# An attention and gated long-convolution kernel: the order of its first loads, tile-wise loads of later batches, and a new written-out order

## The chip, the cores and the metric

The kernel runs on one core of one Trainium2 chip, as one program. The metric is the device time of one execution in microseconds. The core has five engines that run side by side, each through its own list of instructions in order: TensorE (PE in the profile, its weight loads PEld), VectorE (DVE), ScalarE (ACT), GpSimd (POOL) and SyncE (SP). GpSimd and SyncE issue most of the transfers here; a transfer that changes the type from fp32 to fp16 on its way is issued by GpSimd, one that copies as it is by SyncE.

## The reference, cut to what matters

Four batches of 768 rows go through attention of 8 heads with 64 columns each, and then through a gated long convolution over the rows:

```python
scores = scale * q @ k^T + bias          # bias = -slope[head] * distance
keep   = (column < 8) | (0 <= row - column < 96)
a      = softmax(where(keep, scores, -1e9))
x      = a @ v                           # [4, 768, 8*64]
proj   = x @ w_proj                      # [4, 768, 3*512] -> x1, x2, x3
conv   = irfft(rfft(x2) * rfft(filter))  # along the 768 rows
out    = (x1 * conv * x3) @ w_out        # fp32
```

The inputs are fp32; the kernel computes in fp16 with fp32 sums.

## The kernel before

**Tiling.** A batch's attention works on four head pairs (0 to 3) and three column groups. `turned` (L623) transposes the q and the k of a head pair on TensorE, six 128-row tiles each, and copies them to QT and KT. `scores` (L651) makes a pair's scores of one group; in batch 0 the distances (the array `dg`) are multiplied in on TensorE ahead of them ("near"), in later batches the exponentials are multiplied with a mask on VectorE. ScalarE takes the exponential to E. `values` (L695) multiplies with v and normalizes into xn, `transpose_x` (L744) turns the result to xT, and `butterfly` (L764) makes the sums and differences that the transform needs. `gate` and `gates` make x1 and x3 and their product; `conv` (L867) does the projection of x2, the transforms as matmuls with sine tables, the product with the filter's spectrum, the way back, the product with the gates and the output projection, whose results go out by SyncE.

**The order.** Every operation is recorded in a graph with its predecessors (`Plan.op`). A text, `ORDER` (L41), then lists all of them by number and engine: `50V` is operation 50 on VectorE. The four digits behind a P are PSUM banks, and `i3b6` means three dummy matmuls into bank 6 that only keep TensorE busy. Each engine runs its own operations in the text's order, and nothing is moved at run time. Copies that can run on VectorE or ScalarE get their engine from the text too. So an operation that waits holds up all that stand behind it on its engine.

**The first loads.** `load_pair` (L336) loads q and k of a head pair. For batch 0 and pairs 0 and 1 SyncE loads them as fp32 into staging places of their own (parts of h1, h2 and pp) and a "cast" on VectorE copies them to qn and kn (L307). All other q and k loads are issued by GpSimd, one head at a time, 768 rows of 64 columns (96 KB as fp16). The layout of qn and kn is [128 rows, 4 pairs, 6 tiles, 2 heads, 64]. `load_run` and `load_rows` load v by tiles of 120 rows, `load_w` the projection's weights, and the filter is one load of 768 KB into g. GpSimd also makes row numbers (L382), the identity (L199 of a library) and the first step of the distances (`distances`, L514 to L523), whose place in GpSimd's list is behind its first five loads: k, k, q, q of heads and the filter. SyncE's list begins with q and k of pair 0 or 1 into pp, q into h1, the first v rows of batch 0 into X, and k into h2.

**Later batches.** `load_batch` (L1079) calls `load_pair` for the four pairs of the next batch, and `load_v`. A transpose of one pair can start when the two heads of that pair have landed.

Of the kernel before, what the change touches and what calls it, by code (L numbers as in the profile page):

```python
# [17 lines left out]
P = 128  # L18
NG = 8
KL = P - NG  # L20
# [24 lines left out]
106P01 29V 105A 68G 6V 35V 107A 156P67 88P4 8V 157A 31V 69G 89V 123A 124P01 120P45 70G 214V 215V 71G 102P67  # L45
100P2 121A 74G 158P45 216V 103A 125A 249G 98P3 101V 154P67 159A 99V 64S 235G 155A 108P23 126P45 110P67 217V
250G 160P01 218V 109A 127A 219V 111V 220V 112V 238G 161A 247G 75G 248G 115P23 128P45 133P67 227P0 113P1 116V
72G 83A 117V 134V 85A 129V 241G 225P2 237G 135V 118P3 162P67 130V 167P45 73G 114V 131P1 27A 228A 226A 81A 28V
80A 206P2 163V 223P0 164V 132A 168V 136P1 236G 165P6 240G 169V 221P7 119V 166V 84A 170P3 189V 245G 246G 137A
209V 82A 242G 224A 79A 146P6 150P1 152A 171V 229P45 239G 352P3 151P1 222A 188V 244G 243G 197V 213A 211A 76G  # L50
191V 353A 350P7 147P0 251G 231V 180P5 148V 184P3 198V 351A 153V 230A 149V 385P01 199V 190V 182A 363P67 200V
207V 476G 201V 386A 475G 364A 142P4 138P5 186A 340P0 259G 254G 338P1 232P67 212A 341A 192V 144V 193V 202V 233A
194V 387V 339V 143P3 210A 203V 185P4 140A 176P6 256G 252S 354P01 208A 145V 423P23 234A 187V 178V 196V 414P45
355A 415A 255G 344P7 342P6 195V 139P0 348P1 345V 257G 343V 424A 356V 365V 204V 141V 181P7 474G 349A 379P23
473G 357P45 346P6 347V 461G 462G 258G 472G 172P1 183V 177P0 358A 484G 376P45 417P67 380A 359V 174A 360P23 205V
179V 377A 274P1 425V 261P0 253S 418A 361A 381V 420P67 382P45 416V 362V 265P2 421A 383A 469G 275A 263P3 471G
264A 371P45 378V 419V 422V 366P67 384V 289P1 372V 367V 262A 173P3 373V 466G 287P0 266A 388P45 368V 175V 290A
389V 288A 291V 374P2 269P6 267P7 369P3 375A 270A 268A 278P0 276P2 370A 463G 279A 577P3 393P01 390V 277A 280P2
292V 578A 271V 575P7 272V 470G 394V 576A 426P45 273V 465G 281A 282P3 477G 283A 391P6 395V 431P01 396P7 392A
397A 701G 427V 588P23 480G 428V 301P4 432V 285V 433V 589A 429P5 468G 464G 284V 410P7 430A 467G 573P6 434P0  # L60
482G 610P23 406P5 302A 571P4 706G 590V 574A 611A 305P6 699G 435V 306A 286V 695G 297P0 298A 303P1 412A 572V
295P2 453V 293P4 299P3 452V 296A 307P6 481G 308A 694G 294A 304A 300V 485G 563P0 398P7 698G 402P6 585P23 408A
400A 455V 567P1 404A 310V 309V 607P45 407P7 586A 691G 454V 686G 311V 564A 568A 608A 403P6 569P2 411P3 405V
570A 440P6 399P1 456V 565P0 442A 312V 457V 582P45 409V 696G 478S 609V 458V 401V 566A 645P67 646A 693G 583A
436P2 459V 413V 499P0 639P67 640A 486P1 313V 692G 500A 479S 437P3 697G 460V 314V 438A 487A 587V 601P67 604P45
501P2 690G 483G 439V 444P3 315V 612V 602A 687G 605A 579P67 647V 648P01 709G 446A 502A 603V 448P4 642P23 580A
643A 584V 606V 688G 445P5 794P6 618P23 649A 641V 792P7 795A 447V 596P01 793A 644V 581V 597V 700G 450A 619V
503P5 504A 796P6 788P7 598V 613P01 620V 316V 591P23 800P5 614V 260G 689G 514P4 789A 449P7 797A 507P6 592V 615V
651P01 515A 801A 508A 593V 505P2 650V 317V 867P45 318V 506A 594P3 798P6 451V 868A 490P2 799A 595A 656P45 319V
657V 652V 802P7 488P6 491A 658V 803A 616P2 441P3 599P7 659P4 489A 617A 621P6 510V 492P5 653V 509V 600A 512P2  # L70
622A 443V 493A 511V 654P7 494P0 513A 320P6 495A 635P5 707G 321A 813P01 329P2 516V 496V 655A 660A 702G 870P67
869V 814A 637A 330A 636P4 517V 335P0 807P23 677V 638V 678V 871A 497V 808A 832P45 673P1 679V 790P6 520P7 680V
703S 627P2 833A 681V 532P3 704S 521A 632P7 815V 675A 873P45 631P1 533A 682V 791A 332P6 498V 874A 526P3 524P4
708G 629A 705G 633A 522P2 527A 525A 333A 518P1 674P5 834V 683V 875V 685V 336A 322S 523A 628P4 710G 530P6 531A
528P0 676V 684V 634V 519A 630V 323P5 835P23 809V 810P67 529A 804P01 726P4 324A 811A 836A 864P67 711P5 623P2
805A 535V 334S 331S 865A 534V 812V 715P3 536V 826P67 829P01 625A 712A 806V 537V 716A 713P5 830A 821P23 827A
837V 538V 872V 326P0 816P67 727A 737P4 539V 714A 822V 540V 823V 724P1 817V 327A 543V 818A 669P0 866V 541V
843P23 844V 738A 671A 828V 725A 728P5 717P4 729A 730P6 845V 665P7 718A 731A 831V 542V 719P1 739P0 624P5 720A
838P23 626V 740A 667A 670P6 325S 839V 840A 732P0 881P45 722V 672V 544V 876P67 733A 741V 819P1 661P2 662P0 877V
882V 878V 820A 721V 337S 560P1 883A 879P3 824P6 663A 735V 666P7 723V 884P4 548P2 825A 841P6 846P5 885A 742V  # L80
668V 734V 880A 664V 755P4 842A 736V 847A 747P3 557P7 756A 753P6 757P0 902V 751P4 328S 748A 903V 743P3 754A
749P5 758A 752A 905V 750A 745P6 746A 848P0 904V 744A 759V 545P4 852P3 554P6 906V 854A 911P3 546A 924P4 912A
760V 907V 551P3 549A 937P2 925A 850A 761V 908V 762V 849P4 939P0 909V 938A 910V 763V 561A 913P2 547S 851V 555A
764V 562S 940A 558A 914A 857P1 928P0 929A 917P2 915P7 918A 926P0 916A 919P2 927A 941V 920A 853P7 552A 765V
942V 930P0 932P6 766V 860P2 931A 768V 767V 550S 933A 922V 856P3 770P0 921V 858A 935V 553S 556S 923V 934V 773P3
771A 943P0 962P6 862A 774A 947P2 944A 948A 855V 936V 861P4 769V 963A 958P0 945P5 949P2 959A 964P3 863V 946A
950A 960P6 772S 776P0 779P2 965A 961A 859V 775S 777A 951V 952V 780A 967V 966V 953V 968V 785P6 954V 782P7 969V
559S 955V 890P2 898P3 970V 956V 778S 900A 971V 781S 887P0 957V 972V 894P1 886P3 973V 783A 892A 975V 974V 786A
976V 988V 896V 899P2 986V 977P6 978A 895P7 888A 983P1 897V 984A 784S 901V 787S 891P7 889V 980P6 981A 893V 979S
989V 985S 987V 999P6 993P7 1000A 982S 994A 1001S 995S 996P6 997V 990P0 998S 991A 992S  # L90
# [108 lines left out]
class Fused:  # L199
# [7 lines left out]
    LATE = frozenset(())  # L207
# [27 lines left out]
    def buffers(self):  # L235
# [5 lines left out]
        self.qn = t("qn", [P, 4, 6, 2, D])  # L241
        self.kn = t("kn", [P, 4, 6, 2, D])
# [32 lines left out]
        self.under = [[("h", 0), ("h", 2)], [("h", 1), ("h", 3)]] + [[(x, i) for x in ("p1", "p2") for i in range(2)]] * 2  # L275
        self.y = t("y", [P, 4, S])
# [43 lines left out]
    def load(self, eng, dst, src, w, nbytes, name, r=()):  # L320
        self.loads += 1
        e = {"G": self.nc.gpsimd, "S": self.nc.sync}[eng]
        return self.g.op(eng, 0.57 + 0.00035 * nbytes[0] if eng == "G" else 0.5, lambda _: e.dma_start(dst, src),  # L323
                         w=w, r=r, nbytes=nbytes, name=name, bias=-2000.0 + self.loads)
# [14 lines left out]
    def load_pair(self, b, hp):  # L339
        for i, (what, x, dst) in enumerate((("q", self.q, self.qn), ("k", self.k, self.kn))):  # L340
            to = dst[:, hp]
            if b or hp not in self.PLAIN:
                for hh in range(2):
                    self.load("G", to[:, :, hh], x[b, 2 * hp + hh].rearrange("(t p) d -> p t d", p=P),
                              [(what + "n", hp, hh)], (768, 256), f"{what}{hp}")
# [3 lines left out]
            self.load("S", st, x[b, 2 * hp:2 * hp + 2].rearrange("h (t p) d -> p (h t) d", p=P),  # L349
                      own[0:1], (1536, 256), f"{what}{hp}")  # L350
            st = st.rearrange("p (h t) d -> p t h d", h=2)
# [16 lines left out]
    def load_w(self, o, n):  # L368
        wr = self.w_proj.rearrange("(t p) n -> p t n", p=P)
        self.load("G", self.w[:, :, o:o + n], wr[:, :, o:o + n],  # L370
                  [("w", i) for i in range(o // P, (o + n) // P)], (512, 4 * n), f"w{o}")
# [791 lines left out]
```

## Time and profile before

| what | value |
|---|---|
| runs | 170.92, 172.21, 172.63 us; median 172.21 |
| the profiled execution | 171.85 us, of which the span of the profile is 170.1 |
| TensorE busy | 160.6 us (94%), 1614 matmuls |
| VectorE busy | 155.9 us (92%) |
| ScalarE busy | 150.2 us (88%) |
| GpSimd busy | 81.9 us (48%), nearly all of it issuing loads |
| mean granted TensorE clock | 0.99 |

The profile comes from one execution. "Busy" is the union of the instructions' durations; a matmul's duration includes its way through the array, so a busy TensorE is not one at its peak. A row of the timeline is start, duration, engine, line, operation and shapes; in brackets stands the idle time of the engine just before, and what ended it. A row of the windows is a stretch, its length, each engine's busy time with its instructions (PE, PEld, DVE, ACT, POOL, unless one engine alone is asked for), the granted TensorE clock, the DMA share and the GB/s moved. A row of groups ends in busy time, mean ns of one | idle time before them.

### The profile page before, as it was taken

How to read it: one execution, taken by the hardware profiler on the slowest of the kernel's cores; microseconds unless marked ns; L12 is line 12 of the kernel's file. 1: busy time of each engine (PE TensorE's matmuls, PEld its weight loads, DVE VectorE, ACT ScalarE, POOL GpSimd, SP SyncE). 2: the span in 40 equal slices, each digit the busy share in tenths (PEclk: the TensorE clock that was granted, in tenths of full speed). 3: DMA queues.
4: the chain of work that ended last, by engine and by line, in shares of the span. 5: the costliest groups of instructions: out<-in, count | busy, mean ns of one | idle time of the engine just before them, and what ended most of it. 6: DMA issues, size and time to landing. Idle time of an engine off the chain costs nothing. (4 is left out here: it accounts for less than half of the span.)

```text
span 170.1 us, 4259 instructions
## 1 busy us (share of the span) xinstructions
PE 160.6 (94%) x1614; PEld 96.2 (57%) x1614; DVE 155.9 (92%) x364; ACT 150.2 (88%) x308; POOL 81.9 (48%) x107
## 2 busy tenths in 40 slices
PE   7795998999999999999999999999999999999981
PEld 2452347766655688555677546646577644565540
DVE  5993789999999999999999999999999999999950
ACT  5779499999999999999999999999999789894441
POOL 8997999999799899999940000000000000000000
PEclk9999599999999999999999999999999999999999
DMA  6999999999999999999999110330100013343344
GB/s 133 194 200 190 154 158 166 176 160 161 157 158 136 130 111 135 121 133 112 135 148 91 14 62 4 123 123 14 51 2 4 0 62 123 129 185 123 149 186 158
DMA packets 87139, 20.30 MB, mean 119 GB/s; under 512 B 79872, under 2 KB 84176, under 8 KB 87120
## 3 DMA queue, kind: packets, MB, share of 16 engines
q0 software_dynamic: 76976, 11.84, 95.5%
q1 hardware_dynamic: 10144, 8.20, 15.6%
q8 instruction: 12, 0.20, 0.5%
q14 instruction: 7, 0.06, 0.1%
HBM read 25.25 MB, written 6.29 MB: 185 GB/s over the span
## 5 line engine op out<-in xcount | busy, mean ns | idle before, releaser
L832 PE MATMUL bank<-xT,w 128*128 128x384 f16 x256 | 49.1, 326 | 0.0
L674 ACT ACTIVATE E<-bank 128x864 f16<-128x864 f32 x48 | 41.8, 952 | 2.5 <-PE bank L663 2.5
L832 PEld LDWEIGHTS <-w 128*128 128x128 f16 x256 | 23.5, 98 | 16.3 <-issue 1.1
L323 POOL DMA_DIRECT2D vn<-in_v_dram x28 | 26.1, 959 | 2.5 <-DMA g<-in_moe_filter_fft_dram 1.4
L323 POOL DMA_DIRECT2D kn<-in_k_dram x28 | 24.0, 869 | 0.8 <-PE bank L629 0.7
L946 PE MATMUL bank<-wo,y 128*128 128x512 f16 (+1 forms) x100 | 23.7, 370 | 0.7 <-DVE y L995 0.7
L323 POOL DMA_DIRECT2D qn<-in_q_dram x28 | 23.8, 864 | 0.3 <-PE bank L917 0.2
L691 DVE TENSOR_TENSOR E<-E,mask 128x864 f16<-128x864 f16 x36 | 20.4, 595 | 0.0
L311 ACT ACTIVATE ot<-bank 128x512 f32<-128x512 f32 (+1 forms) x24 | 14.9, 636 | 5.4 <-PE bank L946 4.8
L311 ACT ACTIVATE x<-bank 128x384 f16<-128x384 f32 x28 | 15.8, 590 | 3.6 <-PE bank L832 3.4
L846 DVE TENSOR_TENSOR g<-bank,x 128x384 f16<-128x384 f32 x32 | 17.0, 547 | 0.5 <-ACT X L307 0.3
L733 DVE TENSOR_TENSOR xn<-bank,rc 128x512 f16<-128x512 f32 (+1 forms) x21 | 15.9, 771 | 0.1
L890 PE MATMUL bank<-w,xs 128*128 128x512 f16 x64 | 16.0, 379 | 0.0
L709 PE MATMUL bank<-vn,E 128*128 128x65 f16 x224 | 15.2, 193 | 0.7 <-DVE xn L733 0.5
L663 PE MATMUL bank<-QT,KT 64*128 64x216 f16 (+2 forms) x224 | 15.6, 248 | 0.0
L714 PE MATMUL bank<-vn,E 128*128 128x65 f16 x192 | 15.0, 193 | 0.0
L946 PEld LDWEIGHTS <-y 128*128 128x128 f16 x100 | 9.5, 98 | 9.6 <-DVE y L995 1.2
L709 PEld LDWEIGHTS <-E 128*128 128x128 f16 x224 | 13.9, 97 | 1.5 <-issue 0.3
L307 ACT CAST X<-bank 128x512 f16<-128x512 f32 x24 | 14.7, 732 | 0.0
L663 PEld LDWEIGHTS <-KT 64*128 64x128 f16 x224 | 7.8, 95 | 12.0 <-issue 10.8
L714 PEld LDWEIGHTS <-E 128*128 128x128 f16 x192 | 13.2, 97 | 1.7 <-issue 1.1
L307 ACT COPY KT<-bank 128x720 f16<-128x720 f16 (+2 forms) x36 | 13.6, 524 | 0.2 <-PE bank L629 0.2
(156 smaller groups left out, 343.6 us busy)
## 6 DMA issues: line engine op xcount, KB each, us to landing
out_dram<-ot SPq DMA_DIRECT2D x23, 256.0 KB, 2.0
vn<-in_v_dram POOLq DMA_DIRECT2D x28, 120.0 KB, 6.3
kn<-in_k_dram POOLq DMA_DIRECT2D x28, 96.0 KB, 5.2
qn<-in_q_dram POOLq DMA_DIRECT2D x28, 96.0 KB, 4.9
w<-in_moe_w_proj_dram POOLq DMA_DIRECT2D x4, 256.0 KB, 6.4
g<-in_moe_filter_fft_dram POOLq DMA_DIRECT2D x1, 768.0 KB, 11.3
w<-in_moe_w_proj_dram POOLq DMA_DIRECT2D x1, 512.0 KB, 7.4
wo<-in_moe_w_out_dram POOLq DMA_DIRECT2D x1, 512.0 KB, 8.1
```

The lines of the kernel that those rows point to most:

```text
L307: {"A": nc.scalar.copy, "V": nc.vector.tensor_copy, "G": nc.gpsimd.tensor_copy}[e](out, in_)
L311: self.nc.scalar.mul(out, in_, c)
L323: return self.g.op(eng, 0.57 + 0.00035 * nbytes[0] if eng == "G" else 0.5, lambda _: e.dma_start(dst, src), w=w, r=r, nbytes=nbytes, name= ...
L663: nc.tensor.matmul(bs[hh].f32()[:, off:off + w], self.KT[hs, hp, P * m:P * m + P], self.QT[hs, hp, KL * m:KL * m + w], start=(off == 0 and ...
L674: g.op("A", act(864), lambda _: nc.scalar.activation(eo, bs[0].two()[:, :, 0:432].rearrange("p h (m w) -> p h m w", m=2), Act.Exp, scale=s ...
L691: g.op("V", dve(864, 2), lambda _: nc.vector.tensor_mul(eo, eo, mk), r=[("mask", 2 * hp), ("mask", 2 * hp + 1)], w=[("E", hp, gi)], name=" ...
L709: nc.tensor.matmul(o[:, n, hh], ef[:, at:at + P], vt[:, t, 2 * hp + hh, 0:D + 1], start=first, stop=(t == 0), skip_group_check=True)
L714: nc.tensor.matmul(o[:, n, hh], ef[:, at:at + P], vt[:, t - 1, 2 * hp + hh, 0:D + 1], start=False, stop=True, skip_group_check=True)
L832: nc.tensor.matmul(bk.f32()[:, 0:h], self.w[:, c, o + P * j:o + P * j + P], self.xT[:, c, h * s:h * s + h], start=(c == 0), stop=(c == 3))
L846: g.op("V", dve(h, 1, True), lambda _: nc.vector.tensor_mul(x3, pts[1].f32()[:, 0:h], x1), use=[pts[1]], r=[key], w=[ko], name="g")
L890: nc.tensor.matmul(bk.f32(), src[:, c], w[:, c, DM:2 * DM], start=(c == 0), stop=(c == 3))
L946: nc.tensor.matmul(bk.f32()[:, 0:n], y[:, c, P * t:P * t + P], self.wo[:, c, cs], start=(c == 0), stop=(c == 3))
```

## The change

1. GpSimd's loads of batch 0, of the weights and of the filter get the first step of the distances as a predecessor (`after=self.ahead`). In GpSimd's list the distances now stand right behind the row numbers, then the identity, then the filter's load, one q load, the distances' small last step, the other seven q and k loads of pairs 2 and 3, and v.
2. qn and kn have the layout [128 rows, 6 tiles, 512]. Later batches are loaded by `load_tiles`: one load for 128 rows of all 8 heads (1024 rows of 64 columns), 6 for q and 6 for k a batch, where there were 8 and 8 loads of one head. A transpose of any pair then needs all six tiles of its q or k.
3. The pairs that SyncE loads for batch 0 stay 0 and 1 with the same staging places. SyncE's new order is k1, q0, k0, q1 (the digit is the pair), then the first v rows.
4. `CROSS` and `cross` (transposes by DMA) are new, but the set of batches that use them is empty.
5. `ORDER` is new throughout: other places, other banks, 27 dummy matmuls where there were 11, and other engines for some copies (on VectorE 9 qT where there were 6, 10 xT for 5, 17 xn for 21, 4 ot for 1, 1 X for 0, 3 x for 4, 0 eo for 1, 5 slopes for 3, the twin table, and two more parts of the inverse tables).

```diff
-        self.qn = t("qn", [P, 4, 6, 2, D])
-        self.kn = t("kn", [P, 4, 6, 2, D])
+        self.qn = t("qn", [P, 6, DM])
+        self.kn = t("kn", [P, 6, DM])
...
-    def load(self, eng, dst, src, w, nbytes, name, r=()):
+    def load(self, eng, dst, src, w, nbytes, name, r=(), after=()):
...
-                  (8 * KL * n, 256), f"load{what}{t}")
+                  (8 * KL * n, 256), f"load{what}{t}", after=self.ahead)
...
+    def load_tiles(self, b):
+        sides = [("q", self.q, self.qn, P, 0, range(0, self.S, P)), ("k", self.k, self.kn, P, 0, range(0, self.S, P))]
...
+        for n in range(7):
+            for what, x, dst, rows, low, starts in sides:
+                if n < len(starts):
+                    lo = starts[n]
+                    self.load("G", dst[low:P, n].rearrange("p (h d) -> p h d", h=self.H),
+                              x[b, :, lo:lo + rows, :].rearrange("h p d -> p h d"),
+                              [(what + "n", n, h) for h in range(8)], (8 * rows, 256), f"{what}{n}")
...
-        g.op("G", 2.5, first, w=["dg"], bias=-9970)
+        self.ahead = [g.op("G", 2.3, first, w=["dg"], bias=-9970)]
...
-                nc.tensor.transpose(b.f16()[:, P * t:P * t + P], buf[:, hp, t].rearrange("p h d -> p (h d)"), self.ident)
-        g.op("P", pe(*[P] * 6), turn, acq=[b], r=["ident", (what + "n", hp, 0), (what + "n", hp, 1)], name=what)
+                nc.tensor.transpose(b.f16()[:, P * t:P * t + P], buf[:, t, P * hp:P * hp + P], self.ident)
+        self.turns.append(g.op("P", pe(*[P] * 6), turn, acq=[b], r=["ident"] + [
+            (what + "n", t, 2 * hp + hh) for t in range(6) for hh in range(2)], name=what))
...
+        self.distances()
         for i in range(4):
-            self.load_pair(0, i)
-            if i == 0:
-                self.distances()
+            self.load_pair(i)
...
     def load_batch(self, b):
-        for i in range(4):
-            self.load_pair(b, i)
+        self.load_tiles(b)
         self.load_v(b, range(7))
```

The beginning of the order, up to the first scores ("near" is 104 in the old text, 120 in the new):

```diff
-0V 1V 2A 49S 11V 3G 5V 4V 7G 9V i3b6 17P0 46V 44A 18A 12P1 19V 55G 51S 56G 20V 43A 54G 13A 45A 42A 50V 22P2
-47A 38V 14V 15V 23A 32S 52V 10V 41V 16A 53G 77G 24V 36G 90P3 39G i1b6 92P1 61S 60G i3b6 96P0 59G 48V 25V 58G
-57G 30V 91A 67G 33V i4b6 86P2 93A 37V 65G 62A 21A 40V 94P1 26A 66G 104P45 87A 97V 34S 122P23 78A 63V 95V
+0V 1V 2A 4V 3G 5V i2b6 17P0 9V 51S 52V 45S 22P1 32G 12P2 33V 47S 46V 13A 7G 34V 23A 14V 38V 37A 18A 48V 15V
+49S 61S 8V 92P3 50V 86P4 87A 77G 19V 57G 39A i3b6 88P4 20V i4b6 90P2 16A 35G 55G 24V 53G 11V 56G 36V 93A 91V
+21A 40V 43V 89A i7b6 120P45 25V 214V 42V 62A 29V 26A 31V 121A 44V i2b0 206P1 54G 215V 102P23 122P67 84A 103A
```

In the new text 52, 46, 48 and 50 are the casts of k1, q0, k0 and q1, 32 and 35 the distances' first and last step on GpSimd, 33 and 36 those on VectorE, 14, 15, 19, 20, 24 and 25 the angles of the sine tables, 16, 21 and 26 the sines, 77 the filter's load, 92, 86, 88 and 90 the transposes of k1, q0, k0 and q1, 93 and 89 the copies of KT, 121 the first exponential.

More of the change, by code (lines that the diff above doesn't have):

```diff
@@ L275, in buffers @@
         self.under = [[("h", 0), ("h", 2)], [("h", 1), ("h", 3)]] + [[(x, i) for x in ("p1", "p2") for i in range(2)]] * 2
+        self.turns = []
         self.y = t("y", [P, 4, S])
@@ new lines, in cross @@
+    def cross(self):
+        nc, S = self.nc, self.S
+        loads = [x for x in self.g.ops if "G" in x.cost and x.bytes]
+        for n in range(7):
+            for what, src, dst, ok in (("k", self.kn, self.KT, True), ("q", self.qn, self.QT, n < 6)):
+                if not ok:
+                    continue
+                gis = [gi for gi, ms in enumerate(self.GRP) if (n in ms if what == "k" else any(
+                    KL * m < P * n + P and KL * m + self.EW[m] > P * n for m in ms))]
+                out = dst[:, :, P * n:P * n + P]
+                self.g.op("S", 1.3, lambda _, out=out, src=src, n=n: nc.sync.dma_start_transpose(out, src[:, n]),
+                          r=[(what + "n", n, h) for h in range(8)] + ([("kg", 0 if n < 2 else 2)] if what == "k" else []),
+                          w=[(what + "T", n)], nbytes=(128, 1024), name="xbar",
+                          after=loads + [x for gi in gis for x in self.before[gi]])
@@ L370, in load_w @@
         self.load("G", self.w[:, :, o:o + n], wr[:, :, o:o + n],
-                  [("w", i) for i in range(o // P, (o + n) // P)], (512, 4 * n), f"w{o}")
+                  [("w", i) for i in range(o // P, (o + n) // P)], (512, 4 * n), f"w{o}", after=self.ahead)
     def setup(self):
@@ L1063, in load_first @@
         self.load("G", self.fl, self.filt.rearrange("(t p) n -> p t n", p=P),
-                  [("g", 1, j, s) for j in range(4) for s in range(2)], (768, 2048), "filter")
+                  [("g", 1, j, s) for j in range(4) for s in range(2)], (768, 2048), "filter", after=self.ahead)
     def first_rows(self, vt):
```

134 lines of the change are left out of this document (76 added, 58 removed).

## The prediction

> **What bounds the kernel now.** I read the windows first, then the waits, then the start of each queue.
>
> ```profile
> core 0: us, PE busy (x) PEld busy (x) DVE busy (x) ACT busy (x) POOL busy (x), PEclk, DMA share, GB/s
> 16.00:163.47 147.47, 145.22 (x1522) 89.10 (x1522) 144.31 (x311) 136.54 (x283) 67.23 (x79) 0.99 1.13 111
> 163.47:170.10 6.63, 2.77 (x16) 1.49 (x16) 0.43 (x2) 1.58 (x3) 0.00 (x0) 1.00 0.43 162
> ```
> ```profile
> 16.00 0.56 DVE L307 CAST kn<-h 128x768 f16<-128x768 f32 x1 [2.25 <-DMA h<-in_k_dram]
> ...
> 162.46 1.01 DVE L995 TENSOR_TENSOR y<-y,g 128x768 f16<-128x768 f16 x2
> ```
>
> From 16.00, where VectorE starts the last of four casts of the first batch, to 163.47, where it ends the last product, it is busy for 144.31 of 147.47 us. TensorE looks as full and ScalarE nearly so; I take VectorE for the bound, since its gaps are the smallest for work that can't overlap on one engine as TensorE's does (the second rival takes the other side). So I treat it as a queue: the end is the moment at which its steady run begins, plus the work still in its queue, plus its gaps, plus 6.63 us of projection, copy and store. The start decides what is left, and one wait ends it:
>
> ```profile
> DVE kn L307 <- DMA h<-in_k_dram: 2.3, 1, 2.3
> ```
> ```profile
> g<-in_moe_filter_fft_dram POOLq DMA_DIRECT2D x1, 768.0 KB, 11.3
> ...
> h<-in_k_dram SPq DMA_DIRECT2D x1, 384.0 KB, 10.6
> ```
> ```profile
> 5.41 0.39 SPq L323 DMA_DIRECT2D h<-in_k_dram  x1
> ```
>
> The last of SyncE's four big loads is issued at 5.41 and lands 10.6 us later, at 16.0. The columns of the two DMA rows are the size and the time from issue to landing. The filter, which GpSimd issues at 5.61 (its row follows), lands 11.3 us later, at 16.9.
>
> **The change: when the last SyncE load lands.** The new order puts GpSimd's distances ahead of its loads; the first load is then the filter, and SyncE issues k1, q0, k0, q1 (pair numbers), then the few v rows.
>
> ```profile
> 1.37 0.23 POOL L384 IOTA eo<- 1x128 f16 x1
> 1.55 0.19 POOL masks.py:197 MEMSET ident<- 128x128 f16 x1
> 1.82 0.29 POOL masks.py:199 TENSOR_SCALAR_AFFINE_SELECT ident<-ident 128x128 f16<-128x128 f16 x1
> ...
> 5.61 0.84 POOL L323 DMA_DIRECT2D g<-in_moe_filter_fft_dram  x1
> 6.44 0.36 POOL L516 IOTA eo<- 128x216 bf16 x1
> ...
> 8.61 0.23 POOL L523 TENSOR_SCALAR_AFFINE_SELECT eo<-eo 128x48 bf16<-128x48 bf16 x1
> ```
> ```profile
> L323 POOL DMA_DIRECT2D kn<-in_k_dram x4: 838/853/1042, 72.2 to 74.8; - x4
> ...
> DMA to landing us min/median/max: 3.1/3.4/3.5
> ```
> ```profile
> 2.00:4.50 2.50, 2.50 (x10) 0.91 (x9) 1.64 (x8) 1.39 (x6) 2.50 (x4) 1.00 1.15 242
> 11.00:15.00 4.00, 3.89 (x40) 1.66 (x37) 2.47 (x17) 3.58 (x5) 4.00 (x6) 1.00 1.23 200
> ```
>
> GpSimd's row numbers end at 1.60; the distances run from 6.44 to 8.84, 2.40 us; the identity takes 0.5 us. So the filter is issued at 1.60 + 2.40 + 0.5 = 4.5. A load of 96 KB lands at the earliest 3.1 us after its issue, of which its own data are some 0.6 us, so the filter's data begin near 4.5 + 2.5 = 7.0. Until then SyncE has the transfers to itself. At 242 GB/s from 2.0 on it has moved 1.21 MB by 7.0. Its four loads are 4 x 0.393 = 1.57 MB. Three are in by then (1.18 MB); nearly all of q1 (0.36 MB) is not.
>
> What the filter does to a SyncE load beside it, the old trace shows:
>
> ```profile
> L323 POOL DMA_DIRECT2D qn<-in_q_dram x2: 838/896/953, 3.9 to 4.7; - x2
> ...
> DMA to landing us min/median/max: 5.8/6.0/6.2
> ```
> ```profile
> 9.07 0.53 DVE L307 CAST qn<-h 128x768 f16<-128x768 f32 x1
> ```
>
> The cast of the third SyncE load began at 9.07 without a wait, so the fourth, 1.6 us of data by the 242 GB/s, needed up to 16.0 - 9.1 = 6.9 us. GpSimd's load ahead of the filter landed at 4.7 + 6.2 = 10.9, and the filter 6.0 us after it. They went side by side and ended within a microsecond of each other. New order: 0.79 MB of filter and 0.36 MB of q1 from 7.0, at the 200 GB/s of 11 to 15 us, are 5.8 us, and the next GpSimd load (96 KB, 0.5 us) shares with what is left of q1: 13.3. Ends: 8.5 (q1 not slowed at all, 0.36 MB at 242 GB/s), and 14.6 (the 6.9 us of the old case from 7.0, plus the 0.7 us by which I may be wrong on the filter's start). I take 13.3, near the upper end, because the one SyncE load that met the filter behaved so.
>
> The Trainium skill, "DMA: Bandwidth & Descriptors", section Queues, rings and completion order, says that each DMA engine takes turns between queues, a packet from each. By that rule SyncE's queue has no precedence and q1 lands near the filter's end, 13.3; without it, 8.5. The trace agrees: 16.0 beside 16.9.
>
> **What waits behind it.** VectorE's new order puts the cast of q1 (fourth) ahead of two angle tables, the row that completes the distances, and everything after; it is reached by about 9. On TensorE the transposes of q1 stand ahead of the first scores, and the sine and kT copies on ScalarE stand behind tables that VectorE makes after the cast. So all three stop until 13.3. The old order stood only from 13.75.
>
> **VectorE's queue at that moment.** Work that the old order ran before 16.0, the new one has behind the fourth cast: an angle table; gaps, slopes, another angle table, ones; the KT and QT copies, global v rows, a sign row and the fold's parts. These fill three windows:
>
> ```profile
> 3.69:4.65 0.96, 0.96 (x4) 0.29 (x2) 0.72 (x2) 0.69 (x3) 0.96 (x2) 1.00 1.33 233
> 7.20:9.07 1.87, 1.80 (x9) 0.92 (x9) 1.79 (x8) 1.66 (x5) 1.64 (x6) 1.00 1.96 158
> 10.97:13.75 2.78, 2.78 (x28) 1.25 (x26) 2.50 (x17) 2.37 (x3) 2.78 (x4) 1.00 1.22 198
> ```
>
> VectorE: 0.72 + 1.79 + 2.50 = 5.0 us. Then the new order moves copies between VectorE and ScalarE: on VectorE +3 qT, +5 xT, +1 X, two slopes, a twin table, two inverse tables, against -4 xn, -1 x, -1 eo (and +3 ot, in the last 6.6 us, beside TensorE).
>
> ```profile
> L307 DVE COPY QT<-bank 128x768 f16<-128x768 f16 x6 | 3.3, 546 | 0.4 <-PE bank L629 0.4
> L307 DVE COPY xT<-bank 128x480 f16<-128x480 f16 x2 | 0.8, 398 | 0.0
> L733 DVE TENSOR_TENSOR xn<-bank,rc 128x512 f16<-128x512 f32 x14 | 9.2, 684 | 0.0
> L313 DVE TENSOR_SCALAR x<-bank 128x384 f16<-128x384 f32 x4 | 2.2, 546 | 0.0
> ```
>
> Neighbours overlap by some 0.08 us, so: 3 x 0.47 + 5 x 0.32 + 0.60 (X, by xn's row, which has its shape) + 1.1 for the five small ones (each 0.1 to 0.35) - 4 x 0.60 - 2 x 0.47 = +1.4 us. Between nothing and 2.5 of this counts, as the gaps of 3.2 us in the long window could hold some; I take 1.4, as that window is 98% busy.
>
> The gaps:
>
> ```profile
> DVE KT L307 <- PE bank L629: 0.9, 1, 0.9
> ```
>
> This wait for a late k pair, and 0.1 of smaller ones, go: -1.0. They could stay (0) if the scores, all still to come at 13.3, starve it.
>
> **Parts that I cost at nothing.** GpSimd's later loads by tiles: 12 instead of 16 a batch for the same bytes; it issues beside everything. Sixteen more dummy matmuls: TensorE waits for q1 in most of them, and the seven ahead of the first scores lie beside ScalarE's sines. The layout of qn and kn changes no instruction's size. If that cover is gone the price stands under the third rival.
>
> **The sum**, against the profiled execution's own 171.85 us (span 170.1): queue at the start of the steady run +5.0 + 1.4, that start earlier by 16.0 - 13.3, -2.7, gaps -1.0: 171.85 + 2.7 = 174.55, say **174.5**. The three runs have their median 0.4 above the profiled one; I leave that out. Bounds: 172.0 (q1 at 13.3, no net work, gaps -2.2) to 178.0 (all dear ends at once: 14.6, 2.5, gaps 0).
>
> **Rivals.**
> 1. *q1 isn't slowed.* It lands at 8.5, VectorE reaches its cast at 9 and never stops: start -7.0 in place of -2.7, 174.5 - 4.3 = **170.2**. It needs the filter's data to begin 1.5 us later than I think, or SyncE to be served first. The point from which it decides: equal to before at q1 landing by 10.6 (16.0 - 5.4). For it: three loads alone do come quicker. Against it: the row of the one load that met the filter. The Trainium skill, "SBUF — State Buffer", section SBUF: two separate sides, says VectorE's fast copies can keep GpSimd from writing a DMA's descriptors, which would delay the filter; in the window from 10.97 VectorE is at work for 2.50 of 2.78 us beside GpSimd's loads, and no issue is seen stretched here (kn's mean is 0.87 us, below). Chance 0.20.
> 2. *VectorE isn't the bound but TensorE.* TensorE's 145.22 in the long window is as full. Its work is the same but for dummies, so the net 1.4 and 0.6 of the moved work fall away: **172.5**. Against it: TensorE's busy time covers waits in its pipeline. Chance 0.12.
> 3. *Tiles of all heads come late.* A batch's first k transpose needs all six k tiles, not one pair.
>
> ```profile
> L323 POOL DMA_DIRECT2D vn<-in_v_dram x28 | 26.1, 959 | 2.5 <-DMA g<-in_moe_filter_fft_dram 1.4 <-DMA w<-in_moe_w_proj_dram 1.1
> L323 POOL DMA_DIRECT2D kn<-in_k_dram x28 | 24.0, 869 | 0.8 <-PE bank L629 0.7
> ...
> 34.90 0.50 PE L629 MATMUL bank<-ident,kn 128*128 128x128 f16 x6
> ```
>
> GpSimd from 4.5: filter 0.8, eight loads 7.0, a mask 1.0, seven v 6.7, then seven tiles at 1.0 (v's 0.96 for 960 rows; a tile has 1024) and two weights at 0.8: 28.6; landing by the 6.2 us of the q load above: 34.8. TensorE came to this point at 34.9 before and would come at 37.4 now. If GpSimd slips by over 2.6 us, every microsecond counts in full: 2 us give **176.5**. Chance 0.12.
> 4. *The move does nothing*: the transfers are full until all v is in, either way, and the new order only reshuffles: **171.9**. Chance 0.06.
>
> **Numbers.** About 1% is what a measurement here tells from no change: faster is below 170.5, slower above 173.9, by the median 172.21. The forecast has 0.50 (0.42 slower, 0.08 within). Rival 1: 0.15 faster, 0.05 within. Rival 2: 0.10 within, 0.02 slower. Rival 3: 0.12 slower. Rival 4: 0.06 within. So faster 0.15, within 0.29, slower 0.56. The range from 169.9, a little under rival 1, to 176.6, rival 3, leaves out some 0.15.
>
> **What would show it.** In the new profile: VectorE waiting for a SyncE load of q until 12 to 14.5, with TensorE and ScalarE idle beside it; the filter landing in the same microseconds; the first exponential five to six microseconds behind q1 (cast, tables, sines, table load); then VectorE without gaps. Wrong would be: that wait missing or over by 10.6; long gaps of VectorE after 30; or TensorE waiting for qn or kn tiles from 30 on.

## The result, and the profile after

The changed kernel takes 183.15 us (median of four runs, 182.37 to 184.55); the kernel before takes 172.42 beside it. The ratio is 1.066, with a 95% interval from 1.056 to 1.077. The profiled execution of the changed kernel took 183.05 us with a span of 181.2, so the span has grown by 11.1 us from 170.1. The forecast was 174.5.

VectorE's waits in the changed kernel (the total, the number of waits and the longest, in us):

```profile
DVE qn L308 <- DMA pp<-in_q_dram: 4.9, 1, 4.9
DVE KT L308 <- PE bank L664: 3.1, 2, 2.4
DVE kn L308 <- DMA pp<-in_k_dram: 2.6, 1, 2.6
DVE rc L778 <- PE bank L754: 1.6, 2, 1.3
```

The first row is the wait that the forecast named, VectorE waiting for q1. In the second and fourth VectorE waits for TensorE (transposes of k, then sums of the values), 4.7 us together; all its waits for matmuls into a bank come to 7.6 us now and came to 1.5 before. The load of q1 among the DMA issues of the changed kernel (size, time from issue to landing):

```profile
pp<-in_q_dram SPq DMA_DIRECT2D x1, 384.0 KB, 11.3
g<-in_moe_filter_fft_dram POOLq DMA_DIRECT2D x1, 768.0 KB, 8.5
```

q1 was issued at 3.96 and landed at 15.3; the filter, issued at 3.92, landed at 12.4. So q1 came 2.0 us later than the forecast's 13.3, and 0.7 outside its bounds.

Where the 11.1 us are shows best when the span is cut at two events that both kernels have: the first matmul of the first scores ("near"), and the first butterfly on VectorE. The windows of the kernel before, cut there:

```profile
core 0: us, PE busy (x) PEld busy (x) DVE busy (x) ACT busy (x) POOL busy (x), PEclk, DMA share, GB/s
0.00:11.78 11.78, 9.52 (x50) 4.61 (x51) 9.46 (x42) 7.90 (x19) 10.72 (x24) 1.00 1.28 174
11.78:33.22 21.44, 19.04 (x252) 10.56 (x250) 17.21 (x50) 18.73 (x26) 19.60 (x24) 0.92 2.00 170
33.22:170.10 136.88, 132.07 (x1318) 81.02 (x1315) 129.22 (x274) 123.58 (x265) 51.60 (x61) 1.00 0.96 107
```

And those of the changed kernel:

```profile
0.00:19.52 19.52, 12.01 (x50) 5.26 (x51) 9.85 (x39) 8.16 (x19) 15.85 (x31) 0.87 1.48 169
19.52:41.10 21.58, 19.94 (x259) 11.19 (x258) 15.39 (x55) 17.64 (x27) 13.94 (x17) 0.96 1.52 110
41.10:181.20 140.10, 134.20 (x1324) 81.91 (x1322) 132.10 (x282) 124.83 (x281) 43.60 (x49) 1.00 0.92 104
```

The second column is the length of each stretch. The scores start 7.7 us later. From there to the first butterfly both kernels need the same, 21.4 and 21.6 us, although VectorE is busy for 17.2 of them in the one and 15.4 in the other, so it isn't full in either (of the 4.2 us missing before, 2.5 lie ahead of 16.0, nearly all in the wait for k0). From the butterfly to the end the changed kernel needs 3.2 us more. The sum is 7.74 + 0.14 + 3.22 = 11.1. So there are two things to explain: the late scores, and the 3.2 us. The same cut is made for the runs below. Some executions are slower, at a lower granted clock: the ratios below leave them out, the medians count them, and of run 8, whose profile is of one, only the kind of its waits is read.

What stands ahead of the scores, in TensorE's timeline of the changed kernel, and the clock granted to TensorE in stretches of 2 us (the column after the busy time):

```profile
15.92 0.82 PE L664 MATMUL bank<-ident,qn 128*128 128x128 f16 x6 [4.34 <-DVE qn L308]
16.53 3.19 PE L304 MATMUL bank<-uw 128*128 128x512 f16 x7
19.52 0.93 PE L693 MATMUL bank<-eo 128*128 128x432 bf16 x2
```
```profile
14.00:16.00 2.00, 0.08 (x2) 0.62 2.23 153
16.00:18.00 2.00, 2.00 (x10) 0.50 2.41 153
18.00:20.00 2.00, 2.00 (x7) 0.50 2.41 152
20.00:22.00 2.00, 2.00 (x16) 0.67 2.41 152
```

TensorE stands idle for 4.34 us until q1 is there, transposes it, and works off seven dummies (L304) at half the clock in 3.2 us before the scores of pair 0 begin, for which q1 isn't needed.

Finally the longest of GpSimd's waits in the changed kernel (two, of 12.1 us together, the longer 7.6):

```profile
POOL kn L324 <- PE bank L664: 12.1, 2, 7.6
```

A tile of k of the next batch overwrites the place of all four pairs. So GpSimd stops for 7.6 us, from 21.3 to 28.95, until the last pair of batch 0 is transposed.

### The profile page after: what moved, and what is told of

Read it like the earlier page. It is cut to its first block, busy times and chain, and to the rows that moved or that the text cites. A ratio compares the mean times of both kernels' runs of the same rounds, so it can differ in the third digit from the quotient of the medians.

```text
span 181.2 us, 4287 instructions
## 1 busy us (share of the span) xinstructions
PE 166.2 (92%) x1630; PEld 98.4 (54%) x1630; DVE 157.3 (87%) x375; ACT 150.6 (83%) x325; POOL 73.4 (41%) x95
## 3 DMA queue, kind: packets, MB, share of 16 engines
q1 hardware_dynamic: 10144, 8.20, 15.3%
## 4 chain that ended last, share of the span: by engine, by line
PE 37%; ACT 35%; DVE 13%; DMA 6%; issue 4%; SPq 2%; DVEq 0%; ACTq 0%
ACT E L714 12%; PE bank L872 9%; PE bank L991 8%; DMA pp<-in_q_dram 6%; ACT ab L312 4%; ACT xn L777 4%; PE bank L935 4%; ACT X L308 3%; PE bank L304 3%; ACT KT L308 3%; DVE E L731 3%; ACT x L312 2%; PE bank L794 2%; PE bank L664 2%; SPq L324 2%
## 5 line engine op out<-in xcount | busy, mean ns | idle before, releaser
L872 PE MATMUL bank<-xT,w 128*128 128x384 f16 x256 | 48.6, 326 | 0.1
L714 ACT ACTIVATE E<-bank 128x864 f16<-128x864 f32 x48 | 41.1, 946 | 1.7 <-PE bank L699 1.7
L324 POOL DMA_DIRECT2D kn<-in_k_dram x22 | 19.9, 915 | 17.8 <-PE bank L664 12.1
L991 PE MATMUL bank<-wo,y 128*128 128x512 f16 (+1 forms) x100 | 23.1, 370 | 0.0
L324 POOL DMA_DIRECT2D qn<-in_q_dram x22 | 19.7, 929 | 0.8 <-PE bank L664 0.8
L749 PE MATMUL bank<-vn,E 128*128 128x65 f16 x224 | 15.7, 193 | 0.9 <-DVE xn L773 0.6
L312 ACT ACTIVATE ot<-bank 128x512 f32<-128x512 f32 x21 | 12.4, 625 | 4.6 <-PE bank L991 4.3
L754 PE MATMUL bank<-vn,E 128*128 128x65 f16 x192 | 15.5, 193 | 0.0
L699 PE MATMUL bank<-QT,KT 64*128 64x216 f16 (+2 forms) x224 | 15.3, 244 | 0.1
L308 ACT CAST eo<-bank 128x384 f16<-128x384 f32 x32 | 14.8, 546 | 0.0
L308 ACT CAST X<-bank 128x512 f16<-128x512 f32 x23 | 13.9, 676 | 1.0 <-PE bank L1051 1.0
L754 PEld LDWEIGHTS <-E 128*128 128x128 f16 x192 | 13.3, 97 | 1.8 <-issue 1.2
L777 ACT ACTIVATE xn<-bank,rc 128x64 f16<-128x64 f32 x60 | 14.2, 509 | 0.0
```

Source lines behind the costliest of these rows:

```text
L308: {"A": nc.scalar.copy, "V": nc.vector.tensor_copy, "G": nc.gpsimd.tensor_copy}[e](out, in_)
L312: self.nc.scalar.mul(out, in_, c)
L699: nc.tensor.matmul(bs[hh].f32()[:, off:off + w], self.KT[hs, hp, P * m:P * m + P], self.QT[hs, hp, KL * m:KL * m + w], start=(off == 0 and ...
L714: g.op("A", act(864), lambda _: nc.scalar.activation(eo, bs[0].two()[:, :, 0:432].rearrange("p h (m w) -> p h m w", m=2), Act.Exp, scale=s ...
L749: nc.tensor.matmul(o[:, n, hh], ef[:, at:at + P], vt[:, t, 2 * hp + hh, 0:D + 1], start=first, stop=(t == 0), skip_group_check=True)
L754: nc.tensor.matmul(o[:, n, hh], ef[:, at:at + P], vt[:, t - 1, 2 * hp + hh, 0:D + 1], start=False, stop=True, skip_group_check=True)
```

## The experiments

Four causes were on the table. *Late start*: q1 lands late, and all behind its cast moves with it. *Slow clock*: the idle wait leaves TensorE at half its clock. *Tile loads*: GpSimd's wait of 7.6 us makes the loads of batch 1 late. *The order itself*: it has its own gaps whenever the work begins. The forecast's own model, VectorE's queue, is tested from the second set of runs on. All runs compute the whole reference. The table gives each run's median, its ratio to the kernel before measured beside it with the 95% interval, and the three stretches of its profile (start to first scores, to first butterfly, to the end).

| run | median, us | ratio | stretches, us |
|---|---|---|---|
| before | 172.42 | | 11.78, 21.44, 136.88 |
| changed | 183.15 | 1.066 (1.056 to 1.077) | 19.52, 21.58, 140.10 |
| 1 filter behind three loads | 178.83 | 1.047 (1.039 to 1.055) | 13.93, 22.38, 139.99 |
| 2 dummies in the wait | 181.23 | 1.061 (1.055 to 1.066) | 18.22, 21.11, 139.97 |
| 3 no dummies behind q1 | 179.57 | 1.050 (1.044 to 1.056) | 17.87, 22.07, 137.36 |
| 4 batch 1's k elsewhere | 183.84 | 1.066 (1.055 to 1.076) | 18.89, 21.05, 141.06 |
| 5 pair 0 first | 177.49 | 1.035 (1.028 to 1.042) | 12.89, 22.67, 139.64 |
| 6 before, k0 first | 175.69 | 1.022 (1.013 to 1.032) | 17.82, 19.65, 136.93 |
| 7 as 5, no late dummies | 174.69 | 1.019 (1.013 to 1.026) | 12.89, 22.62, 136.99 |
| 8 before, filter behind | 171.49 | 1.001 (0.996 to 1.006) | |
| 9 as 7, waits filled | 173.38 | 1.018 (1.011 to 1.026) | 12.38, 21.54, 137.48 |
| 10 as 9, scores earlier | 173.87 | 1.019 (1.012 to 1.027) | 11.49, 23.05, 138.06 |
| 11 as 10, batch 1's k elsewhere | 173.51 | 1.018 (1.011 to 1.024) | 11.49, 23.01, 137.50 |

**1. The filter behind three of GpSimd's loads.** In the order's text:

```diff
-87A 77G 19V
+87A 19V
...
-24V 53G 11V
+24V 53G 77G 11V
```

> The filter's load is moved in GpSimd's list from the first place to behind three of the q and k loads of pairs 2 and 3; nothing else changes. Late start (the filter's packets hold q1 back, and all behind q1's cast moves with it): q1 lands at 8.5 to 10 instead of 15.3, VectorE and TensorE don't stop, and the time falls by 5 to 6 us, to about 177.5. The order itself is slow (its gaps of VectorE after 20 us come whenever the work begins): the start moves by as much, but under 2 us of it are left at the end, 181 to 183. No precedence (q1 is late for another reason, as GpSimd's small loads): q1 lands later than 13 and the time stays at 183.

The windows of this run, and VectorE's cast of q1 in its timeline with its new wait for the filter:

```profile
0.00:13.93 13.93, 10.87 (x49) 4.75 (x50) 8.98 (x37) 6.97 (x17) 10.72 (x25) 1.00 1.18 161
13.93:36.31 22.38, 19.74 (x258) 11.12 (x258) 16.57 (x58) 18.71 (x29) 18.90 (x23) 1.00 1.99 152
36.31:176.30 139.99, 134.18 (x1325) 81.92 (x1322) 132.06 (x282) 124.74 (x281) 43.56 (x49) 1.00 0.92 105
```
```profile
10.54 0.89 DVE L308 CAST qn<-pp 128x768 f16<-128x768 f32 x1 [0.59 <-DMA pp<-in_q_dram]
17.80 0.96 DVE L600 TENSOR_TENSOR pp<-g 128x1536 f16<-128x1536 f16 x1 [3.14 <-DMA g<-in_moe_filter_fft_dram]
```

q1 is there at 10.5 in place of 15.3, the clock stays at 1.00, and the scores start 5.6 us earlier. That the filter's load in the first place held q1 back is shown. The span falls by 4.9 us, the ratio by 1.9 points. VectorE now stands 3.1 us for the filter, and the second stretch grows by only 0.8, so VectorE seems to have room there. The third stretch, 139.99, doesn't move: its 3.2 us belong to the order.

**2. Dummies that fill the wait.** In the text, `i4b6 90P2` becomes `i24b6 90P2`.

> Twenty more dummy matmuls ahead of the transposes of q1, so that TensorE works through most of the wait that ends at 15.9. Slow clock (the idle wait of 4.3 us leaves TensorE at a granted 0.50 for 5.6 us, which delays the first scores and k of pair 2, and VectorE's gaps follow): the granted clock stays at 1.00 from 15 to 22, the first scores start at about 18.0 instead of 19.5, and the time falls by 2 to 4 us, to 179 to 181. Late start alone: the first scores come earlier, but the end doesn't move by more than 1 us. Tile loads: no change.

TensorE's clock and busy time in this run:

```profile
16.00:17.00 1.00, 1.00 (x11) 1.00 2.41 153
18.00:19.00 1.00, 1.00 (x9) 1.00 2.42 154
```

The clock stays at 1.00, and the scores start at 18.2 in place of 19.5. The span falls by 1.9 us, the ratio by 0.6 points (about 1 us) with intervals that overlap. So the slow clock is worth 1 to 2 us at most, a part of the loss and not the cause; by the medians alone it could be nothing.

**3. No dummies behind q1.** `i7b6`, `i2b0`, `i4b2`, `i2b3` and `i3b1` are taken out, 18 matmuls: seven ahead of the scores and eleven behind (the expectation below counts nine).

> The seven dummy matmuls ahead of the first scores and the four later groups (nine more) are taken out. Dummies on the path (the seven take 3.2 us at the slow clock and end 1.5 us after the scores could begin; two later groups wait for banks that ScalarE's copies of X free, 1.4 us): the time falls by 2 to 3 us, to about 180.5. Dummies harmless: no change within 1 us. Dummies needed (without them TensorE idles longer and its clock stays low longer): slower by 1 to 2 us.

The third stretch of this run, and the window from 60 to 70 us, first of the changed kernel and then of this run:

```profile
39.94:177.30 137.36, 132.91 (x1319) 81.36 (x1317) 132.04 (x282) 124.33 (x281) 43.54 (x49) 1.00 0.95 107
```
```profile
60.00:70.00 10.00, 8.57 (x107) 5.53 (x106) 8.51 (x19) 8.72 (x19) 6.64 (x8) 1.00 2.16 137
```
```profile
60.00:70.00 10.00, 9.96 (x153) 7.36 (x151) 9.83 (x22) 10.00 (x26) 6.88 (x9) 1.00 1.90 122
```

With the dummies TensorE is busy for 8.57 of these 10 us and issues 107 matmuls; without them 9.96 and 153 (shifted by the 1.2 us by which this run is ahead there, from 58.84 to 68.84, it is 9.96 and 150). In the changed kernel's timeline the two late groups look harmless, but each has a wait in its brackets:

```profile
64.22 0.59 PE L304 MATMUL bank<-uw 128*128 128x512 f16 x2 [0.80 <-ACT X L308]
68.78 0.81 PE L304 MATMUL bank<-uw 128*128 128x512 f16 x3 [0.59 <-ACT X L308]
```

A dummy of these writes into a bank, so it first waits until ScalarE has emptied it (0.80 and 0.59 us), and all real work of TensorE stands behind. The five matmuls of these two groups are the only dummies in the third stretch, and without them it falls by 2.7 us, to 137.4: all but 0.5 of the 3.2. The seven ahead of the scores cost 1.3 us: from q1's cast to the scores it takes 2.9 us in place of 4.2. The time falls by 1.6 points.

**4. The k tiles of batch 1 in a place of their own.** They go to y, which is free then:

```diff
+        kn = self.y.rearrange("p a b -> p (a b)").rearrange("p (a b) -> p a b", a=6) if b == 1 else self.kn
-        sides = [("q", self.q, self.qn, P, 0, range(0, self.S, P)), ("k", self.k, self.kn, P, 0, range(0, self.S, P))]
+        sides = [("q", self.q, self.qn, P, 0, range(0, self.S, P)), ("k", self.k, kn, P, 0, range(0, self.S, P))]
```

> The k tiles of batch 1 get a place of their own (y, which is free then), so that GpSimd need not wait until batch 0's k has been transposed for all pairs. Tile loads (GpSimd stands for 7.6 us from 21.3, and all its loads behind it come late): GpSimd's wait goes, the loads of batch 1 and the weights land some 7 us earlier, and the time falls by 3 to 7 us. Late start or slow clock: GpSimd's wait goes as well, but nothing waited for these tiles, and the time stays within 1 us of 183.

GpSimd's timeline in this run and, for comparison, in the changed kernel:

```profile
21.26 0.92 POOL L324 DMA_DIRECT2D y<-in_k_dram  x1
```
```profile
28.95 0.92 POOL L324 DMA_DIRECT2D kn<-in_k_dram  x1 [7.64 <-PE bank L664]
```

The first tile is issued 7.7 us earlier, and the time is the same within the intervals: 1.066 and 1.066. The tile loads are not the cause, although their wait is the longest of an engine other than SyncE. (The third stretch of this run was 1 us longer than the changed kernel's; why is left open.)

In all four runs the stretch from the first scores to the butterfly took 21 to 22.4 us, whenever it began. That gave a fifth theory, *first scores*: the end follows the moment at which they start. The next runs set it against VectorE's queue.

**5. Pair 0 first.** q1 stays as late as it is, but its cast (50), transposes (90) and copy (91) go behind the first two sets of scores of pair 0. The same edit leaves out five dummies (eight stand ahead of the scores where there were eleven, the two behind them go) and sets KT's copy of pair 0 (89) ahead of a sine:

```diff
-49S 61S 8V 92P3 50V 86P4 87A 77G 19V 57G 39A i3b6 88P4 20V i4b6 90P2 16A 35G 55G 24V 53G 11V 56G 36V 93A 91V
-21A 40V 43V 89A i7b6 120P45 25V 214V 42V 62A 29V 26A 31V 121A 44V i2b0 206P1 54G 215V 102P23 122P67 84A 103A
+49S 61S 8V 92P3 86P4 87A 77G 19V 57G 39A i3b6 88P4 20V 16A 35G 55G 24V 53G 11V 56G 36V 93A
+40V 43V 89A 21A i8b6 120P45 25V 26A 206P1 102P23 121A 50V 90P0 91V 214V 42V 29V 31V 44V 84A 103A 62A 54G 215V 122P67
```

> q1 is as late as in the changed kernel, but nothing of pair 0 stands behind it any more: its cast, transposes and copy go behind the first two sets of scores of pair 0, KT's copy of pair 0 ahead of two sines on ScalarE, and the dummies ahead of the scores from eleven to eight, the two behind them out. First scores (the end follows the moment at which the first scores start, by about 21.6 us to the first butterfly and 140 us from there): the scores start at about 12.5 instead of 19.5, the first butterfly comes at 34 to 35, and the time falls by 6 to 7 us, to 176 to 177. VectorE's queue (the end follows the steady run behind q1's cast plus the work left): VectorE still stops for q1 with some 2.7 us less work behind it, and the time falls by 2.7 us, to 180.5.

```profile
0.00:12.89 12.89, 9.78 (x41) 4.46 (x42) 8.20 (x36) 7.45 (x17) 10.20 (x24) 1.00 1.11 177
12.89:35.56 22.67, 19.39 (x263) 11.39 (x262) 17.51 (x58) 18.27 (x29) 19.23 (x23) 1.00 2.05 149
35.56:175.20 139.64, 133.98 (x1324) 82.05 (x1322) 131.49 (x282) 124.52 (x281) 44.25 (x50) 1.00 0.92 105
```

These are its windows. The scores start 6.6 us earlier, the span falls by 6.0 and the ratio by 3.1 points, more than from the filter's move and with q1's cast still at 14.8:

```profile
14.77 0.88 DVE L308 CAST qn<-pp 128x768 f16<-128x768 f32 x1 [2.53 <-DMA pp<-in_q_dram]
```

So it isn't the landing by itself that costs: it is what the order puts behind it. The dummies were not tried apart from the move, but run 3, without any of the late ones, brings the scores forward by only 1.7 us. The result lies 0.5 us above the range of "first scores"; VectorE still waits 2.5 us for q1 in the second stretch, and run 9, which fills that wait, shortens the stretch by 1.1.

**6. The kernel before with k0 first.** The mirror of it: the transposes of k0, which lands at 16.0, ahead of the scores of pairs 1 and 2.

```diff
-66G 104P45 87A 97V 34S 122P23 78A 63V 95V
-106P01 29V 105A 68G 6V 35V 107A 156P67 88P4 8V 157A 31V 69G 89V 123A 124P01 120P45
+66G 87A 97V 34S 78A 63V 95V
+29V 68G 6V 35V 88P2 8V 31V 69G 89V 104P45 122P23 105A 106P01 107A 156P67 157A 123A 124P01 120P45
```

> The kernel before, with one step moved: the transposes of k0, which lands last at 16.0, stand ahead of the first scores of pairs 1 and 2 on TensorE instead of behind them; VectorE's and ScalarE's lists keep their order up to one copy of KT. First scores: they start at about 17.2 instead of 11.8, the time rises by 5 us, to 176 to 177, or by 6 with a slow clock behind the longer idle wait. VectorE's queue: nothing that VectorE has to do ahead of 16.0 is touched, its steady run still begins at 16.0, and the time rises by less than 1.5 us.

```profile
0.00:17.82 17.82, 10.80 (x56) 5.29 (x57) 11.99 (x57) 10.60 (x21) 15.00 (x29) 0.92 1.42 178
17.82:37.47 19.65, 18.88 (x244) 10.08 (x243) 14.28 (x33) 16.08 (x23) 15.34 (x20) 0.90 1.67 127
37.47:174.40 136.93, 132.13 (x1320) 81.06 (x1316) 129.06 (x274) 123.71 (x265) 51.36 (x60) 1.00 0.96 107
```

Nothing that VectorE has to do ahead of 16.0 was touched, and the kernel before becomes 2.2% slower. The scores start 6.0 us later, 1.8 of which the second stretch makes up, and the third is unchanged to 0.05 us. That is less than "first scores" expected and far from VectorE's queue; the part that is made up shows that the rule isn't one to one. (k0's cast itself comes 0.6 us later, at 16.6. TensorE's clock is a little lower here, 0.92 and 0.90 in the first two stretches beside 1.00 and 0.92 before; run 2 prices a slow clock of that kind at 2 us at most.)

**7. Pair 0 first, and no late dummies.** The edit of run 5, without `i4b2`, `i2b3` and `i3b1`.

> The run with pair 0 first, and the dummies of 34, 64 and 69 us taken out as well. If the two gains add up (the run without dummies was 2.7 us shorter from the first butterfly to the end), the time is 2.5 to 3 us below that run, 173 to 174.5; if that gain hung on the late start, no change beside it.

174.69, 2.8 below run 5: the two gains add up. The third stretch is 136.99, that of the kernel before.

**8. The kernel before with the filter two loads later.** `77G` goes from behind `53G` to behind `59G`.

> The kernel before, with the filter's load two q and k loads later in GpSimd's list. VectorE's queue: k0 lands earlier than 16.0, by 1 to 4 us, VectorE's wait for it goes, and the time falls by up to 2 us, less what VectorE then waits for the filter. First scores: they start at 11.8 as before, k0 isn't needed by them, and the time stays within 0.7 us of the kernel before.

The time is that of the kernel before. The longest of VectorE's waits:

```profile
DVE pp L565 <- DMA g<-in_moe_filter_fft_dram: 3.5, 1, 3.5
```

The wait for k0 is gone, and one for the filter has come in its place. The result fits "first scores", but because of this new wait it doesn't speak against VectorE's queue.

**9 to 11. What is left.** Run 9 takes the edit of run 7, puts six small VectorE operations into its wait for q1, ahead of the cast 50V (`42V 29V 31V 44V 10V 30V 50V`), and two copies of inverse tables (213A, 210V) ahead of the exponentials that they stood behind.

> The run with pair 0 first and without late dummies, with two more moves: six small VectorE operations (2.3 us) that need nothing go into its wait for q1, and two copies of inverse tables on ScalarE and VectorE go ahead of the exponentials that they stood behind, so that the bank they hold is free earlier. The scores start at 12.9 as there. If VectorE's gaps of 20 to 33 us are what is left between this and the kernel before, the first butterfly comes 1.5 to 2.5 us earlier and the time falls to 172 to 173; if only the start of the scores counts, the time stays at 174.7.

Run 10 also moves the last row of the distances (36V) and KT's copy of pair 0 (89A) forward, and has four dummies ahead of the scores where run 9 has eight.

> The same, and the row that completes the distances and KT's copy of pair 0 go ahead of the angle tables and of the copies of pair 1. First scores: they start at about 11.3 instead of 12.9, the end follows by 1 to 1.6 us, 170.5 to 172, level with the kernel before. If the exponentials are held by ScalarE's sines and its table load instead, the scores come earlier, the first exponential stays at 14.2, and so does the end.

Run 11 adds the edit of run 4 to that.

> The same as the run with the scores earlier, and the k tiles of batch 1 in a place of their own. If GpSimd's wait for batch 0's transposes was hidden only because all else was late, its removal now gives 1 to 3 us; if nothing waits for those tiles even now, no change within 1 us.

Run 9 shortens the second stretch by 1.1 us, to 21.54, and its profiled span by as much; the ratios of runs 7 and 9 can't be told apart. Run 10 shows where "first scores" ends. Its scores start at 11.49, but ScalarE's timeline is this:

```profile
12.66 0.67 ACT L475 ACTIVATE fold<-y 128x512 f16<-128x512 f32 x1
13.35 1.28 ACT L714 ACT_TABLE_LOAD   x1
14.64 0.89 ACT L714 ACTIVATE E<-bank 128x864 f16<-128x864 f32 x1
```

The first exponential stands behind the last sine and the table's load, and comes no earlier than in run 9 by more than 0.3 us. Nothing is won: the second stretch grows to 23.05. (Its clock of 0.93 isn't the reason, as run 11 needs 23.01 at a clock of 1.00.) In run 11 the tile loads cost nothing that can be measured either (1.018 beside 1.019), so their wait wasn't hidden only by the late start. No run beats the kernel before; the best repaired versions stay 1.8% above it, and what that rest is (1.3 us of run 9's span, more by the medians) was not settled.

## Why the prediction was wrong

**Right.** VectorE waits for q1, the filter's load is what holds q1 back (run 1), and TensorE and ScalarE stand beside it. The first exponential comes 5.7 us behind q1, where five to six were forecast. The work moved behind the cast was sized fairly well. The long window of before ends with VectorE's last product; the same product of the changed kernel ends at 174.65, and its windows from the cast's start to there, and from there on, are:

```profile
173.64 1.01 DVE L1040 TENSOR_TENSOR y<-y,g 128x768 f16<-128x768 f16 x2
```
```profile
15.30:174.65 159.35, 154.91 (x1578) 93.30 (x1578) 149.32 (x344) 144.44 (x312) 61.36 (x70) 0.98 1.05 101
174.65:181.20 6.55, 2.84 (x17) 1.48 (x16) 2.19 (x5) 0.60 (x1) 0.00 (x0) 1.00 0.63 237
```

VectorE is busy for 149.32 us, 5.0 more than the 144.31 of before; the forecast had 6.4 more.

**The step that failed** is the model at the head of the prediction: VectorE as a queue whose end is the start of its steady run, plus its work, plus its gaps. Term by term, in the span: the start of the run moved by -0.7 where -2.7 was forecast (q1 at 15.3 and not 13.3); the work by +5.0 (+6.4); the gaps, 159.35 - 149.32 = 10.0 beside 3.2, by +6.9 (-1.0); the rest behind the last product by -0.1 (none). The sum is +11.1 against +2.7. By far the largest error, 7.9 us, lies in the gaps; the start adds 2.0, and the work takes 1.4 back. Of the 6.9 us of new gaps 4.7 lie ahead of the first butterfly and 2.2 behind it. The prediction saw that the scores, "all still to come at 13.3", might starve VectorE, and priced that at nothing won instead of something lost. By its own first exponential, five to six us behind 13.3, the exponentials would begin at about 18.8, and they begin at 14.41 in the kernel before; that delay has no term in the sum. The first exponentials of the kernel before and of the changed one:

```profile
14.41 3.21 ACT L674 ACTIVATE E<-bank 128x864 f16<-128x864 f32 x4
```
```profile
20.96 0.89 ACT L714 ACTIVATE E<-bank 128x864 f16<-128x864 f32 x1 [0.27 <-PE bank L699]
```

The model came from one window, 16.00 to 163.47, in which VectorE is 98% busy. That mean hides the window's beginning, up to the first butterfly, where VectorE is busy for 15.52 of 17.22 us (90%) even in the kernel before:

```profile
16.00:33.22 17.22, 15.92 (x223) 9.56 (x224) 15.52 (x38) 14.54 (x22) 15.63 (x19) 0.90 2.16 162
```

And the window starts when the old kernel's scores are already under way. From the scores to the butterfly VectorE is busy for 17.21 of 21.44 us before (80%) and for 15.39 of 21.58 in the changed kernel (71%). What paces this stretch, as far as runs 5, 6 and 10 show, is the chain from scores to exponentials, values, xT and butterfly; which of its links sets the pace was not tried. The old order had begun that chain at 11.78, with pairs 1 and 2, while VectorE waited for k0 of pair 0 until 16.0; what that wait cost is not known, since run 8 put another in its place. The new order lets the same chain begin only behind q1. Runs 5 and 6 show it from both sides: with q1 late and pair 0 ahead of it the span falls by 6.0 us, and one step moved in the kernel before costs it 4.3. With the row of the first scores the sum would have been: start at 13.3 + 4.2 (the measured way from the cast to the scores) = 17.5, 5.7 later than 11.78, so about 177.6; q1's two more microseconds make it 179.6.

**The parts costed at nothing.** The dummies weren't free, and the price that the prediction says stands under the third rival is one of tiles alone. The prediction let the seven ahead of the scores lie beside ScalarE's sines; at half the clock they took 3.2 us, and 1.3 of it lay on the path. And two groups at 64 and 69 us, not looked at, wait for banks and cost 2.7 us (run 3), which are most of the rest.

**The rivals.** That q1 isn't slowed (0.20) is refuted by its landing. That the tiles come late (0.12) had a true mechanism with the wrong price: the prediction let the first k tile follow v without a wait and overlooked that it overwrites all pairs; GpSimd waited 7.6 us, the tiles were late, and without that wait the time was the same (runs 4 and 11). TensorE as the bound (0.12) may be nearer in the second stretch, where it is busy for 19.94 of 21.58 us, but it was argued from the long window too, and gave 172.5. That the move does nothing (0.06) is refuted.

## What to carry to other kernels

Before calling an engine the bound, cut the span at events of the computation and look at its busy share in each stretch: a mean of 98% over 147 us hid a beginning of 90%, and from the first scores to the first butterfly the share was 80% before and 71% after. When a load is going to be late, ask first what the order puts behind it that doesn't need it; moving three steps aside, with a few dummies less, was worth at least as much here as making the load early. A filler instruction that needs a buffer is a wait like any other, and the longest wait of a busy engine may cost nothing: take it away and see.

## What the hardware showed that was not expected

TensorE's granted clock fell to 0.50 in the idle 4.34 us, at about 14.5 (the mean is 0.74 in the microsecond from 14 and 0.50 in the next), and stayed there until about 21.3, 5.4 us after work began again; matmuls that fill the wait kept it at 1.00 (run 2). The Trainium skill, "TensorE: Matmul & The Clock Gate", section Part 1: The HAM clock gate, has the clock halved after at least one idle window of about 3.4 us. This trace agrees only in part: the whole wait is longer than that, but the clock fell 2.9 us into it. The kernel before doesn't agree. There the longest idle time ahead of the fall is 1.72 us, from 14.89 to 16.61, with TensorE at work for 0.89 and 1.29 us of the two stretches around it, and the clock falls all the same:

```profile
14.00:16.00 2.00, 0.89 (x12) 1.00 1.48 201
16.00:18.00 2.00, 1.29 (x12) 0.88 2.40 154
18.00:20.00 2.00, 1.96 (x8) 0.50 2.39 149
```

So a wait well under that window, with little work on both sides, was enough; the clock was at 0.50 from about 17.5 to 20.9.

The filter's load also held q1 longer than the prediction reckoned, which let both end together: q1 landed 2.9 us behind the filter, between GpSimd's next two loads. The packets of the two queues show what happened (q0 is GpSimd's, q1 SyncE's; packets, MB, share of the DMA engines), first from 7 to 8 us, then from 7.0 to the filter's landing at 12.42:

```profile
q0 software_dynamic: 161, 0.16, 103.3%
q1 hardware_dynamic: 164, 0.04, 26.2%
```
```profile
q0 software_dynamic: 1118, 0.82, 99.5%
q1 hardware_dynamic: 833, 0.21, 28.5%
```

In most microseconds the queues move about as many packets each (155 beside 153 from 10 to 11, 267 beside 274 from 11 to 12; from 8 to 9 it is 200 beside none, from 9 to 10 163 beside 67). But the filter's packets are of 1 KB here and SyncE's of 256 bytes, so SyncE's queue gets about a fifth of the bytes as long as the filter runs. The last 0.24 MB of q1 then go beside as many bytes of GpSimd's small loads, until 15.3. The prediction shared out bytes, and let only one of the small loads stand beside the rest. It also had three of SyncE's loads in by 7.0; the third, k0, landed at 8.3.
